# Chunked mLSTM with a feed-forward layer: the gates of four chunks in one batch on 128 partitions, and exponents, splits and state product moved behind square, copy of x and y

## The chip, the cores and the metric

The kernel runs on one core of a Trainium2 chip. The metric is the device time of one execution in microseconds, as the median of several runs. The profile is that of one execution. PE is TensorE (PEld its weight loads), DVE is VectorE, ACT is ScalarE, POOL is GpSimd, and SP is SyncE, which here issues the DMA transfers.

## The reference

For 4 batches of 8 heads (32 sequences) of 768 steps with heads of 40 numbers, an mLSTM recurrence is computed, and its output goes through a feed-forward layer of 2048 units.

```python
for t in range(S):
    m_new = np.maximum(f_gate[:, :, t] + m, i_gate[:, :, t])
    f_stab = np.exp(f_gate[:, :, t] + m - m_new)
    i_stab = np.exp(i_gate[:, :, t] - m_new)
    C = f_stab[:, :, None, None] * C + i_stab[:, :, None, None] * np.einsum('bhd,bhe->bhde', vt, kt)
    n = f_stab[:, :, None] * n + i_stab[:, :, None] * kt
    y[:, :, t] = sigmoid(o_gate) * (C @ q) / np.maximum(np.abs(n @ q), 1.0)
x = y.transpose(0, 2, 1, 3).reshape(3072, 320)
h = x @ w_in
g = np.where(h >= 1, h, np.where(h <= -1, 0.0, (h + 1) ** 2 / 4))
return g @ w_out
```

## The kernel before, in words

The sequence is cut into six chunks c of 128 steps. One chunk of one batch is a step n = 4c + b, so there are 24 steps. Within a step the recurrence is a masked product of scores and decays plus what the state brings from earlier chunks.

**Gates.** For each chunk `gate_sums` (L193), `gate_tail` (L239) and `gate_exps` (L253) turn the gates of the 32 sequences into maxima m (a scan along the 128 steps), running sums ac and al of the log decays, exponents G (for scaling v, the state and the output), nA (minus the sums, on the steps' partitions) and dec (the decay of the state). Each works on tiles of 32 partitions with 128 columns, assembles four of them in ex, and transposes ex on PE. The sums go to memory as a_d, since every step reads them back spread over 128 partitions (`load_A`, L462, tile Abc, three buffers), and dec goes through dc_d. Chunk 0 has tiles of its own in the front. Chunk 1 is begun in the front (step `g1` of the table STEPS, L55) and ended after the first group of the feed-forward layer. Chunks 2 to 5 are computed beside the feed-forward layer, a few instructions a group, from the groups 2, 13, 28 and 43 on (GATES_AT, L49).

**A step.** `prep` (L475): POOL masks Abc (`select`), ACT turns it into decays with eight exponents (`decay`, L492), POOL scales v (`scale1`). `score` (L509): PE multiplies k and q, DVE multiplies the scores with the decays (Abc again), POOL scales v once more (`scale2`). `main` (L569): PE forms C times q and the masked product, DVE adds them to hv, divides by z, multiplies with the sigmoid of the output gate (sz) and gets y; PE transposes y, ACT copies it to xh in fp32r, DVE writes the rest xl. `carry_on` (L544) forms the new state C out of a product of k and v on PE, a mask on DVE, and the old state scaled by dec on POOL. From step 8 on, except for batch 3, v and the masked scores are split into three bf16 parts on DVE and POOL (`parts3`, L149, tiles v and m).

**The feed-forward layer** goes in six blocks j of 512 rows (four steps), each of 16 groups fc. `mm1` (L674) makes eight matmuls psh of xh, xl with the split weights wh, wl, ACT applies relu and square (tile r), DVE takes maximum and minimum (r). `parts` splits r into gh (ACT) and gl (DVE), and `mm2` (L695), two groups later, makes twelve matmuls pso with oh, ol (four with the unsplit weight in block 0). A block can begin when x of its four steps is there. psh has two banks. The weights arrive as float64 words and are converted during block 0 by ACT, DVE and POOL (`words`, L309: tiles wraw, mg, win, ow).

**Order.** The front, up to the first feed-forward matmul, runs in the order of STEPS. After that the program places step n's parts at the groups that OFFS, LEAD and MLAG give (`slot`, L657), and a scheduler arranges each engine's instructions; `behind` (L416) asks for an instruction to come after one that is kept in `mark`. The engines then work through their instructions in that order.

Of the kernel before, what the change touches and what calls it, by code (L numbers as in the profile page):

```python
# [44 lines left out]
NA = 3  # L45
ST = 0


GATES_AT = (2, 13, 28, 43)  # L49
# [47 lines left out]
def mlstm_ffn_kernel(ctx, tc, qk, qn, vk, og, fi0, fi, w_in, w_out, cst, out):  # L97
# [62 lines left out]
    rst = const.tile([3 * NSEQ, L], F32, name="rst")  # L160
# [32 lines left out]
    def gate_sums(c):  # L193
# [35 lines left out]
        reset = rst[:NSEQ] if c else rst[2 * NSEQ:]  # L229
# [339 lines left out]
    def main(n):  # L569
# [21 lines left out]
        else:  # L591
            prod = [(i, k) for i in range(3) for k in range(3 - i)]
            v = parts3(t["v1"], "v3", (nc.vector, nc.gpsimd))
            for h in range(H):
                if h % 8 == 0:
                    m = parts3(M[:, h:h + 8, :], "m3", (nc.vector, nc.gpsimd))
# [20 lines left out]
        nc.vector.tensor_tensor(out=y.rearrange("p (h d) -> p h d", d=D), in0=hv[:, :, 0:D], in1=sz, op=ALU.mult)  # L617
# [114 lines left out]
    for what in STEPS.split():  # L732
# [4 lines left out]
        elif what == "Lf":  # L737
            load_gates(mid, 1, 2)
# [16 lines left out]
        elif what[0] == "g":  # L755
            run(gate_sums(n))
# [47 lines left out]
    for x in range(NG + LAG):  # L804
        j, fc = divmod(x, NFC)
        if x < NG:
# [12 lines left out]
            if x in GATES_AT:  # L819
                c = 2 + GATES_AT.index(x)  # L820
                load_gates(later, c, c + 1)
                steps = gate_steps(c)
            if x >= GATES_AT[0]:
# [17 lines left out]
_INS = ["qk", "qn", "vk", "og", "fi0", "fi", "w_in", "w_out", "cst"]  # L841


def _layout(q, k, v, i_gate, f_gate, o_gate, moe_w_in, moe_w_out):
# [22 lines left out]

    w = moe_w_in.view(np.int64)
# [26 lines left out]
```

## Time and profile before

| what | value |
|---|---|
| median of 3 runs | 540.07 us (538.07 to 540.72) |
| profiled execution, its own time | 538.07 us |
| its span, first to last instruction | 536.3 us |
| mean granted clock of PE | 0.958 |
| busy PE / DVE / ACT / POOL | 501.1 / 359.7 / 291.5 / 138.8 us |
| DMA traffic read / written | 46.67 MB / 4.04 MB |
| idle time of POOL's mask, ended by a DMA of Abc | 16.1 us in 10 waits |
| idle time of ACT's exponents, ended by POOL's mask | 37.3 us in 14 waits |
| instructions of DVE / ACT / POOL | 669 / 576 / 140 |

A row of a group or a timeline has the start in the span, the duration, engine, line, operation, output and inputs by the program's names, sizes, and in brackets the idle time of that engine just before it and what ended it. Most lines read L80 or L83, since a helper issues the instructions; the tiles tell which is which. Idle time of an engine that is not the bound costs nothing by itself. The granted clock is the share of full speed that PE was given.

### The profile page before, as it was taken

The page shows a single profiled execution, that of the slowest core. Times are in us where ns is not written, and L with a number is a line of the kernel's source. Part 1 is how long each engine was busy: PE and PEld are TensorE (multiplying, and loading weights), DVE is VectorE, ACT ScalarE, POOL GpSimd, SP SyncE. Part 2 cuts the span into 40 slices and gives each one's busy share as a digit, 9 for nine tenths or more (in the row PEclk, how much of TensorE's full clock was granted, in tenths as well). Part 3 has the DMA queues.
Part 4 walks back from the last instruction along what each step waited for, and adds up shares of the span by engine and source line. Part 5 has one row for each costly group of instructions (what it writes and reads, how often), then busy time and mean ns, then how long its engine had stood idle before and what let it go on. Part 6 is the DMA issues. An engine that isn't in the chain of part 4 may idle for free.

```text
span 536.3 us, 8899 instructions
## 1 busy us (share of the span) xinstructions
PE 501.1 (93%) x3396; PEld 427.1 (80%) x3399; DVE 359.7 (67%) x669; ACT 291.5 (54%) x576; POOL 138.8 (26%) x140
## 2 busy tenths in 40 slices
PE   8957999798997999969999979999999999999996
PEld 5735777676786889958888967988988889989986
DVE  5799997678675687748567558885566755544342
ACT  6544964555267464546636527663668444446553
POOL 3147423233352132223131232431231310000000
PEclk9987999899797999988999988999999999999999
DMA  8859454442441123233221233322243000010001
GB/s 245 264 188 303 129 172 146 149 153 91 142 134 19 41 63 103 79 88 93 51 87 56 80 113 120 74 90 77 68 149 135 19 1 2 0 38 13 1 1 50
DMA packets 29647, 51.30 MB, mean 96 GB/s; under 512 B 10124, under 2 KB 20004, under 8 KB 29604
## 3 DMA queue, kind: packets, MB, share of 16 engines
q1 hardware_dynamic: 29604, 50.72, 30.5%
q8 instruction: 27, 0.44, 0.4%
q14 instruction: 16, 0.13, 0.1%
HBM read 46.67 MB, written 4.04 MB: 95 GB/s over the span
## 4 chain that ended last, share of the span: by engine, by line
PE 75%; DVE 7%; ACT 7%; issue 3%; POOL 3%; DMA 3%; SPq 0%; ACTq 0%; POOLq 0%; DVEq 0%
PE psh L80 31%; PE pso L80 27%; PE psa L80 13%; ACT Abc L80 3%; POOL Abc L80 2%; PE psa L83 2%; DMA Abc<-a_d 2%; ACT r L80 1%; PE pso L83 1%; POOL v L80 1%; DVE r L80 1%; PE psh L83 1%; DVE win L80 1%; DVE ow L80 1%; DMA wraw<-in_w_out 1%
## 5 line engine op out<-in xcount | busy, mean ns | idle before, releaser
L80 ACT ACTIVATE r<-psh,half 128x512 f32<-128x512 f32 x96 | 65.2, 684 | 103.2 <-PE psh L80 102.9
L80 PE MATMUL psh<-xh,wh 128*128 128x512 f32 x288 | 107.4, 429 | 14.8 <-DVE r L80 12.2
L80 DVE SCALAR_TENSOR_TENSOR r<-psh,r 128x512 f32<-128x512 f32 x96 | 65.7, 686 | 80.6 <-ACT r L80 80.0
L80 PE MATMUL psh<-xh,wl 128*128 128x512 f32 x288 | 103.6, 414 | 0.0
L80 PE MATMUL pso<-ow,gh 128*128 128x320 f32 x320 | 99.4, 313 | 0.0
L80 PE MATMUL pso<-oh,gh 128*128 128x320 f32 x320 | 99.3, 313 | 0.0
L80 PE MATMUL pso<-oh,gl 128*128 128x320 f32 x320 | 93.3, 313 | 0.0
L80 DVE TENSOR_TENSOR gl<-r,gh 128x512 fp32r<-128x512 f32 x80 | 60.5, 758 | 32.4 <-ACT gh L80 31.9
L80 ACT CAST gh<-r 128x512 fp32r<-128x512 f32 x80 | 49.5, 618 | 48.9 <-DVE r L80 48.5
L80 PEld LDWEIGHTS psh<-xh,wh 128*128 128x128 f32 x288 | 53.1, 199 | 24.9 <-DVE r L80 13.9
L80 ACT ACTIVATE Abc<-Abc,nA 128x128 f32<-128x128 f32 x160 | 49.3, 390 | 37.3 <-POOL Abc L80 37.3
L80 PEld LDWEIGHTS psh<-xh,wl 128*128 128x128 f32 x288 | 56.7, 199 | 14.0 <-DVE m L83 0.4
L80 PEld LDWEIGHTS pso<-ow,gh 128*128 128x128 f32 x320 | 60.7, 190 | 3.4
L80 PEld LDWEIGHTS pso<-oh,gh 128*128 128x128 f32 x320 | 60.7, 190 | 3.3
L80 PE MATMUL psh<-xl,wh 128*128 128x512 f32 x192 | 62.7, 410 | 0.0
L80 ACT ACTIVATE r<-r 128x512 f32<-128x512 f32 x96 | 60.2, 631 | 2.4
L80 PEld LDWEIGHTS pso<-oh,gl 128*128 128x128 f32 x320 | 58.2, 188 | 0.8
L80 POOL TENSOR_TENSOR v<-vk,G 128x328 f32<-128x328 f32 x36 | 29.7, 829 | 67.2 <-issue 43.7
L80 PEld LDWEIGHTS psh<-xl,wh 128*128 128x128 f32 x192 | 37.6, 197 | 8.5
L80 POOL TENSOR_TENSOR C<-C,dec 120x369 f32<-120x369 f32 x16 | 13.7, 856 | 111.0 <-PE psa L80 111.0
L80 PE MATMUL pso<-ow,r 128*128 128x320 f32 x128 | 39.3, 452 | 0.0
L80 DVE TENSOR_TENSOR Abc<-psa,Abc 128x512 f32<-128x512 f32 x40 | 25.9, 680 | 17.8 <-PE psa L80 17.8
(187 smaller groups left out, 728.2 us busy)
## 6 DMA issues: line engine op xcount, KB each, us to landing
Abc<-a_d SPq DMA_DIRECT2D x20, 512.0 KB
raw<-in_qk SPq DMA_DIRECT2D x48, 160.0 KB
vk<-in_vk SPq DMA_DIRECT2D x20, 324.0 KB
wraw<-in_w_in SPq DMA_DIRECT2D x8, 768.0 KB
wraw<-in_w_out SPq DMA_DIRECT2D x8, 640.0 KB
sig<-in_og SPq DMA_DIRECT2D x6, 640.0 KB
out<-r SPq DMA_DIRECT2D x24, 160.0 KB
qn<-in_qn SPq DMA_DIRECT2D x20, 180.0 KB
```

What stands on the lines that cost most here:

```text
L80: r = getattr(self.engine, name)(*args, **kwargs)
L83: r = getattr(self.engine, name)(*args, **kwargs)
```

## The change

**Gates.** Chunks 1 to 4 are computed at once. The maxima scan runs once over 512 columns on 32 partitions, in the front (step `b` of STEPS, after the score product of step 1). Four transfers from SBUF to SBUF spread the maxima over 128 partitions, chunk by chunk (m_b). From there on every instruction works on 128 partitions, four chunks times 32 sequences: `batch_sums` at step `g1`, `batch_tail` and `batch_exps` after the first group. One transfer writes the sums of the four chunks to a_d, four transposes on PE replace the one of ex, and the twelve decay transfers of the four chunks go out together. The gates arrive in two forms, rows over 512 columns (fi_r) and chunks on partitions (fi_b, a new input fib). Only chunk 5 keeps the old path, from group 34 on.

**Order.** Exponents (`decay`) come behind the latest square of r and the latest copy of x. The mask (`select`) of steps from 8 on is issued one slot before the first exponents rather than in the same slot. The state product C and the splits v and m come behind the latest y.

```diff
-GATES_AT = (2, 13, 28, 43)
+JOINED = (4, 5, 6, 7)
+GATES_AT = 34
-    "x11 v1 m10 c w2 u0 m11 w2 E2 A2 x20 ...
+    "x11 v1 m10 c w2 u0 m11 b w2 E2 A2 x20 ...
+    def load_batch():
+        mb["row"] = mid.tile([NSEQ, 2, 4 * L], F32, name="fi_r")
+        nc.sync.dma_start(mb["row"], fi[:, :, L:5 * L])
+        mb["fi"] = mid.tile([P, 2, L], F32, name="fi_b")
+        nc.sync.dma_start(mb["fi"], fib)
+    def batch_maxima():
+        m = mid.tile([NSEQ, 4 * L + 1], F32, name="m_r")
+        nc.vector.tensor_copy(m[:, 0:1], carry)
+        nc.vector.tensor_tensor_scan(out=m[:, 1:], data0=mb["row"][:, 0, :], data1=mb["row"][:, 1, :], initial=m[:, 0:1],
+                                     op0=ALU.add, op1=ALU.max)
+        nc.vector.tensor_copy(carry, m[:, 4 * L:])
+        for c in range(4):
+            nc.sync.dma_start(mb["m"][c * NSEQ:(c + 1) * NSEQ], m[:, c * L:(c + 1) * L + 1])
+    def batch_sums():
...
+        nc.vector.tensor_tensor_scan(out=ac, data0=rst, data1=ah, initial=0.0, op0=ALU.mult, op1=ALU.add)
+        nc.sync.dma_start(a_d[1:5].rearrange("c s t -> (c s) t"), ac)
+    def batch_exps():
+        for q, x in enumerate((mb["fi"][:, 0, :], mb["m"][:, :L], mb["ac"], mb["ah"])):
+            nc.tensor.transpose(tp[:, q * P:(q + 1) * P], x, ident)
+        nc.scalar.activation(Gq[:, 0:3], tq[:, 0:3], AF.Exp)
+        nc.scalar.activation(Gq[:, 3], tq[:, 3], AF.Exp, scale=-1.0)
+        nc.scalar.mul(nA[:, 1:5, :], tq[:, 2], -1.0)
+        nc.scalar.activation(dx, mb["dc"].broadcast_to([P, D]), AF.Exp)
+        nc.sync.dma_start(dc_d[1:5].rearrange("c b (h d) -> (c b h) d", d=D), dx)
+        for g, h0 in enumerate(GROUPS):
+            for c in range(1, 5):
+                nc.sync.dma_start(dec[:, g, :, c], dc_d[c, :, h0 * D:(h0 + 3) * D].rearrange("b x -> x b"))
         select(n)
+        if n not in JOINED:
+            yield
         for hh in range(2):
-            decay(n, hh)
+            with behind(("r", "act"), ("x", "act")):
+                decay(n, hh)
-        nc.vector.tensor_tensor(out=Cn, ...
+        with behind("y"):
+            nc.vector.tensor_tensor(out=Cn, ...
-            v = parts3(t["v1"], "v3", (nc.vector, nc.gpsimd))
+            with behind("y"):
+                v = parts3(t["v1"], "v3", (nc.vector, nc.gpsimd))
-        y = ...
-            todo = ("prep", s0 - (LEAD if j > 1 else LEAD - 1), 3), ...
+            lead = (LEAD if j > 1 else LEAD - 1) + (n not in JOINED)
+            todo = ("prep", s0 - lead, 3 + (n not in JOINED)), ...
             if x == 0:
-                    run(gate_tail(1))
-                    gate_exps(1)
+                    batch_tail()
+                    batch_exps()
```

What this moves is shown at the start of block 2 on three engines. A row is an instruction: line, operation, output and inputs, size. On ACT before, around the copy of x (xh) of the last step that block 2 needs; Abc are the exponents, r the relu or the square, gh the cast of g:

```order
L80 CAST gh<-r 128x512
L80 ACTIVATE ex<-ah 32x128
L80 ACTIVATE Abc<-Abc,nA 128x128 x8
L80 CAST xh<-psa 128x3x128
L80 ACTIVATE r<-psh,half 128x512 x2
L80 COPY r<-pso 128x320
L80 ACTIVATE r<-r 128x512 x2
```

The same place on ACT in the changed kernel:

```order
L82 CAST gh<-r 128x512
L82 ACTIVATE r<-psh,half 128x512
L82 CAST xh<-psa 128x3x128
L82 ACTIVATE Abc<-Abc,nA 128x128 x4
L82 ACTIVATE r<-r 128x512
L82 ACTIVATE Abc<-Abc,nA 128x128 x4
L82 CAST gh<-r 128x512
```

The copy of x stood behind the eight exponents and now stands ahead of them; they have moved behind it, in two halves.

On DVE before, the work of the same step's y (hv, z, sz, y), the state product C, the split v and the rest of x (xl, xh):

```order
L80 TENSOR_TENSOR hv<-psa,hv 128x328
L80 TENSOR_TENSOR C<-psa,cs 120x369
L80 TENSOR_TENSOR v_2414<-v_2194 128x328
L80 SCALAR_TENSOR_TENSOR z<-hv,G 128x8
L80 TENSOR_TENSOR C<-C 120x369
L80 TENSOR_TENSOR z<-z,hv 128x8
L80 RECIPROCAL z<-z 128x8
L80 TENSOR_TENSOR sz<-sig,z 128x320
L80 TENSOR_TENSOR y<-hv,sz 128x320
L80 TENSOR_TENSOR xl<-psa,xh 128x2x128
```

The same on DVE in the changed kernel:

```order
L82 TENSOR_TENSOR hv<-psa,hv 128x328
L82 TENSOR_TENSOR ow<-ow,oh 128x640
L82 SCALAR_TENSOR_TENSOR z<-hv,G 128x8
L82 TENSOR_TENSOR gl<-r,gh 128x512
L82 TENSOR_TENSOR z<-z,hv 128x8
L82 RECIPROCAL z<-z 128x8
L82 TENSOR_TENSOR sz<-sig,z 128x320
L82 TENSOR_TENSOR y<-hv,sz 128x320
L82 TENSOR_TENSOR C<-psa,cs 120x369
L82 TENSOR_TENSOR v_2340<-v_2131 128x328
L82 TENSOR_TENSOR C<-C 120x369
```

C and the split of v (the next step's) stood among z, sz and y, and now follow y.

On PE before, around the transposes of that y (ident,y), the last pso matmuls of block 1 and the first psh matmuls on the new x:

```order
L80 MATMUL pso<-oh,gh 128x320
L80 MATMUL pso<-oh,gl 128x320 x3
L80 MATMUL pso<-ow,gh 128x320
L80 MATMUL pso<-oh,gl 128x320
L80 MATMUL psa<-ident,y 128x128 x3
L80 MATMUL psa<-raw 128x128
L80 MATMUL psh<-xh,wh 128x512 x2
L80 MATMUL psh<-xh,wl 128x512 x2
```

The same on PE in the changed kernel:

```order
L82 MATMUL psh<-xh,wh 128x512
L82 MATMUL psh<-xh,wl 128x512
L82 MATMUL pso<-oh,gh 128x320
L82 MATMUL psa<-ident,y 128x128 x3
L82 MATMUL pso<-ow,gh 128x320
L82 MATMUL psa<-raw 128x128
L82 MATMUL pso<-oh,gl 128x320
L82 MATMUL pso<-oh,gh 128x320
L82 MATMUL pso<-ow,gh 128x320
```

Before, all 24 pso matmuls that follow the step's state product stand ahead of the transposes, and the block's first psh matmuls follow them at once. Now 21 pso matmuls and the last two psh groups of block 1 stand between the state product and the transposes, and 23 pso matmuls between the transposes and block 2's first psh matmul.

More of the change, by code (lines that the diff above doesn't have):

```diff
@@ L96, in mlstm_ffn_kernel @@
 @with_exitstack
-def mlstm_ffn_kernel(ctx, tc, qk, qn, vk, og, fi0, fi, w_in, w_out, cst, out):
+def mlstm_ffn_kernel(ctx, tc, qk, qn, vk, og, fi0, fi, fib, w_in, w_out, cst, out):
     nc = Core(tc)
@@ L158, in parts3 @@
         return hi, mid, lo
-    rst = const.tile([3 * NSEQ, L], F32, name="rst")
+    rst = const.tile([P, L], F32, name="rst")
     nc.gpsimd.memset(rst, 1.0)
@@ new lines, in batch_sums @@
+    def batch_sums():
+        a, m = mb["fi"][:, 0, :], mb["m"]
+        ah = mb["ah"] = mid.tile([P, L], F32, name="ah_b")
+        ac = mb["ac"] = mid.tile([P, L], F32, name="ac_b")
+        nc.vector.tensor_tensor(out=a, in0=a, in1=m[:, :L], op=ALU.add)
+        nc.vector.tensor_tensor(out=a, in0=a, in1=m[:, 1:], op=ALU.subtract)
+        nc.vector.tensor_scalar(out=ah, in0=a, scalar1=CLAMP, scalar2=GRID, op0=ALU.max, op1=ALU.add)
+        nc.vector.tensor_scalar(out=ah, in0=ah, scalar1=-GRID, scalar2=None, op0=ALU.add)
+        nc.vector.tensor_tensor_scan(out=ac, data0=rst, data1=ah, initial=0.0, op0=ALU.mult, op1=ALU.add)
+        nc.sync.dma_start(a_d[1:5].rearrange("c s t -> (c s) t"), ac)
+        nc.vector.scalar_tensor_tensor(out=a, in0=a, scalar=CLAMP, in1=ah, op0=ALU.max, op1=ALU.subtract)
@@ new lines, in batch_tail @@
+    def batch_tail():
+        i, m, ah, ac = mb["fi"][:, 1, :], mb["m"], mb["ah"], mb["ac"]
+        b = mb["fi"][:, 0, :]
+        al = ah
+        nc.vector.tensor_tensor_scan(out=al, data0=rst, data1=b, initial=0.0, op0=ALU.mult, op1=ALU.add)
+        nc.vector.tensor_tensor(out=b, in0=i, in1=m[:, 1:], op=ALU.subtract)
+        nc.vector.tensor_tensor(out=b, in0=b, in1=al, op=ALU.subtract)
+        dh = m[:, :L]
+        nc.vector.tensor_tensor(out=dh, in0=ac[:, L - 1:].broadcast_to([P, L]), in1=ac, op=ALU.subtract)
+        nc.vector.tensor_tensor(out=dh, in0=dh, in1=b, op=ALU.add)
+        nc.vector.tensor_tensor(out=dh, in0=dh, in1=al[:, L - 1:].broadcast_to([P, L]), op=ALU.add)
+        mb["dc"] = mid.tile([P, 1], F32, name="dc_b")
+        nc.vector.tensor_tensor(out=mb["dc"], in0=ac[:, L - 1:], in1=al[:, L - 1:], op=ALU.add)
@@ L616, in main @@
         y = wk.tile([P, DM], F32, name="y", bufs=2)
-        nc.vector.tensor_tensor(out=y.rearrange("p (h d) -> p h d", d=D), in0=hv[:, :, 0:D], in1=sz, op=ALU.mult)
+        mark["y"] = nc.vector.tensor_tensor(out=y.rearrange("p (h d) -> p h d", d=D), in0=hv[:, :, 0:D], in1=sz, op=ALU.mult)
         if 0 < c < NC - 1:
@@ L647, in mlstm_ffn_kernel @@
         if j:
-            todo = ("prep", s0 - (LEAD if j > 1 else LEAD - 1), 3), ("score", s0, 2), ("main", s0 + MLAG, 3)
+            lead = (LEAD if j > 1 else LEAD - 1) + (n not in JOINED)
+            todo = ("prep", s0 - lead, 3 + (n not in JOINED)), ("score", s0, 2), ("main", s0 + MLAG, 3)
         else:
@@ L755, in mlstm_ffn_kernel @@
         elif what[0] == "g":
-            run(gate_sums(n))
+            if n:
+                batch_sums()
+            else:
+                run(gate_sums(n))
+        elif what[0] == "b":
+            batch_maxima()
         elif what[0] == "k":
@@ L818, in mlstm_ffn_kernel @@
                         pass
[L819 to L823, printed above, removed]
+            if x == GATES_AT:
+                load_gates(later, NC - 1, NC)
+                steps = gate_steps(NC - 1)
+            if x >= GATES_AT:
                 with tc.issue_after(mark["r", "dve"].ins):
```

22 lines of the change are left out of this document (15 added, 7 removed), and 2 rows, old and new, of the table STEPS.

## The prediction

> **What bounds the kernel now.** I read the page, then TensorE's waits, then stretches of the span, then single instructions.
>
> ```profile
> span 536.3 us, 8899 instructions
> PE 501.1 (93%) x3396; PEld 427.1 (80%) x3399; DVE 359.7 (67%) x669; ACT 291.5 (54%) x576; POOL 138.8 (26%) x140
> ```
>
> TensorE (PE) is busy for 501.1 of 536.3 us, so any gain here has to come out of the 35.2 us of idle time, or out of time in which its clock is reduced. Both lie in a few stretches. The columns are the stretch, its length, busy time of PE, weight loads, VectorE (DVE), ScalarE (ACT) and GpSimd (POOL), the granted clock, DMA share and GB/s.
>
> ```profile
> 31.00:44.00 13.00, 5.89 (x17) 4.14 (x18) 12.53 (x25) 6.62 (x12) 7.50 (x5) 0.76 0.77 260
> 98.00:105.00 7.00, 4.03 (x25) 3.31 (x25) 6.51 (x11) 2.12 (x6) 2.01 (x3) 0.82 0.54 171
> 105.00:119.00 14.00, 13.92 (x72) 11.43 (x73) 11.03 (x25) 7.24 (x16) 4.93 (x5) 0.84 0.48 147
> 119.00:145.00 26.00, 22.82 (x111) 17.77 (x110) 19.42 (x36) 10.91 (x26) 8.92 (x9) 0.87 0.40 128
> 145.00:161.00 16.00, 15.36 (x133) 13.16 (x131) 12.25 (x26) 9.76 (x16) 8.74 (x5) 1.00 0.45 139
> 161.00:181.00 20.00, 16.70 (x85) 14.19 (x84) 11.41 (x23) 13.19 (x28) 3.20 (x4) 0.83 0.07 11
> 222.00:242.00 20.00, 15.71 (x95) 13.07 (x95) 12.27 (x23) 8.20 (x19) 6.77 (x6) 0.91 0.36 112
> 242.00:305.00 63.00, 63.00 (x495) 55.74 (x494) 42.85 (x81) 35.91 (x73) 17.29 (x18) 0.97 0.24 71
> 305.00:327.00 22.00, 17.48 (x113) 14.71 (x111) 13.79 (x29) 9.71 (x23) 5.87 (x7) 0.92 0.35 107
> 327.00:400.00 73.00, 73.00 (x569) 65.55 (x570) 53.08 (x93) 45.16 (x89) 23.05 (x22) 0.98 0.32 97
> ```
>
> Idle time is length less PE's busy time; what the clock costs is length times what the clock lacks to 1. That gives six terms. (b) 31 to 44: 7.1 us idle. (c) 98 to 119: 3.05 idle and 2.2 of clock, 5.3. (d) 119 to 145: 3.2 and 3.4, 6.6. (e) 145 to 181: 3.9 and 3.4, 7.3. (f) 222 to 305: 4.3 and 3.7, 8.0. (g) 305 to 400: 4.5 and 3.2, 7.7. A dip of the clock follows each wait, so a wait costs nearly twice its length. Terms (c) to (g) hold 34.9 us.
>
> **What makes the waits.** Term (f), at the start of block 2; columns are start, length, engine, line, operation, tiles:
>
> ```profile
> 225.49 0.53 DVE L80 TENSOR_TENSOR C<-psa,cs 120x369 f32<-120x369 f32 x1
> 226.87 0.70 DVE L80 TENSOR_TENSOR z<-z,hv 128x8 f32<-128x8 f32 x1
> 227.84 1.41 DVE L80 TENSOR_TENSOR sz<-sig,z 128x320 f32<-128x320 f32 x1
> 229.28 0.49 DVE L80 TENSOR_TENSOR y<-hv,sz 128x320 f32<-128x320 f32 x1
> 227.81 1.09 POOL L80 TENSOR_SCALAR_AFFINE_SELECT Abc<-Abc 128x1024 f32<-128x1024 f32 x1 [0.27 <-DMA vk<-in_vk]
> 228.94 2.45 ACT L80 ACTIVATE Abc<-Abc,nA 128x128 f32<-128x128 f32 x8 [4.52 <-POOL Abc L80]
> 231.29 0.45 ACT L80 CAST xh<-psa 128x384 fp32r<-128x384 f32 x1
> 229.92 0.52 PE L80 MATMUL psa<-ident,y 128*128 128x128 f32 x3 [2.17 <-DVE y L80]
> 231.80 0.88 PE L80 MATMUL psh<-xh,wh 128*128 128x512 f32 x2 [0.94 <-ACT xh L80]
> ```
>
> Two things hold PE up. DVE runs the state product C and the bf16 split of v before it finishes y, and z and sz stretch beside POOL's work. Then ACT stands 4.52 us in front of eight exponents whose mask POOL has not written yet, and the copy of x, which the block's first matmul needs, is queued behind them. Term (g) is the same picture one block on:
>
> ```profile
> 315.83 0.52 PE L80 MATMUL psa<-ident,y 128*128 128x128 f32 x3 [2.31 <-DVE y L80]
> ```
>
> Terms (d) and (e) show the other half of it:
>
> ```profile
> 132.20 2.67 PE L80 MATMUL psa<-v,Abc 128*128 128x41 f32 x16 [1.93 <-DVE xh L80]
> 155.73 4.72 POOL L80 TENSOR_SCALAR_AFFINE_SELECT Abc<-Abc 128x1024 f32<-128x1024 f32 x1 [3.17 <-DMA Abc<-a_d]
> 160.48 0.99 ACT L80 ACTIVATE Abc<-Abc,nA 128x128 f32<-128x128 f32 x3 [2.16 <-POOL Abc L80]
> 164.81 1.22 PE L80 MATMUL psh<-xh,wh 128*128 128x512 f32 x2 [3.30 <-DVE r L80]
> ```
>
> ACT waits for a mask, the relu and square behind it come late, DVE's r comes late, and PE has no free bank.
>
> **The change part by part.** *Order of exponents, mask, C and splits: terms (c) to (g).* Exponents now stand behind the square and the copy of x, the mask of steps from 8 on is issued a slot earlier, C and the splits stand behind y. The program's order shows it at block 2: C and the v split follow y, the copy of x precedes the exponents, and PE has 21 pso matmuls and two psh groups of eight between the state matmuls and the transposes, and 23 pso matmuls between those and the first matmul on the new x. A group of eight and the twelve pso matmuls that go with it last
>
> ```profile
> 520.90 1.86 PE psh L80 x8
> 522.76 1.75 PE pso L80 x12
> ```
>
> so y now has two times 1.86 and 21 times 1.75/12 us of work to cover it, 6.8 us, and the copy of x 23 times 1.75/12, 3.4 us. From C at 225.49 to the end of y at 229.77 DVE took 4.3 us with the work that now goes behind; the way from the transposes to the first matmul took 1.9. Both are covered, so I take three quarters of (f) and of (g): -6.0 and -6.0. The quarter left is for what comes late next, the score product and its split. Block starts (d) and (e) lose the same cause, but there the weight conversions share DVE, ACT and POOL, and a step's mask can still come late; I take half: -3.3 and -3.5. Bounds for each of the four are nothing and the whole term.
>
> Term (c) begins with the gates of chunk 2 and the queue of SP:
>
> ```profile
> 85.46 1.34 DMA dc_d<-dx
> 88.76 4.10 DMA Abc<-a_d
> ```
>
> The load of the sums for step 7 stood behind the decay transfers of that chunk. These are gone from there, which frees the 3.3 us from 85.46 to 88.76; of 5.3 I take -3.0, bounds 0 and -5.3.
>
> *Gates in a batch.* Four chunks at 128 partitions take as many instructions as one did at 32, so three sets go. On DVE they lie where PE is bound, except at the start, term (b):
>
> ```profile
> 34.36 1.23 DVE L83 TENSOR_TENSOR_SCAN m<-fi_t,m 32x128 f32<-32x128 f32 x1
> 36.36 1.55 DVE L83 TENSOR_TENSOR fi_t<-fi_t,m 32x128 f32<-32x128 f32 x2
> 41.51 0.40 DVE L83 TENSOR_TENSOR_SCAN ah<-rst,fi_t 32x128 f32<-32x128 f32 x1
> 42.72 0.69 DVE L80 SCALAR_TENSOR_TENSOR r<-psh,r 128x512 f32<-128x512 f32 x1
> 43.46 1.22 PE L80 MATMUL psh<-xh,wh 128*128 128x512 f32 x2 [6.80 <-DVE r L80]
> ```
>
> DVE is full here and PE waits for r. The maxima scan goes to the front, and the last scan stands behind the first r: 1.23 and 0.40 less ahead of r, 1.6 at most; the two subtractions stay, though earlier. I take -1.5, bounds 0 and -1.6.
>
> The front pays: a scan over 512 columns ahead of the first z, at most four times 0.40, 1.6 us, overhead counted four times, which leaves room for its two one-column copies.
>
> ```profile
> 17.76 0.49 DVE L83 TENSOR_TENSOR y<-psh,sz 128x320 f32<-128x320 f32 x1
> 19.24 0.53 PE L83 MATMUL psa<-ident,y 128*128 128x128 f32 x3
> ```
>
> y ends at 18.25 and PE takes it at 19.24, so 1.0 of it is hidden: +0.6, bounds 0 and +1.6. The four transfers of maxima leave when that scan ends, near 20, and are first read at about 32; at 4.1 us, the longest row above, 8 us are left. SP holds its later loads until then, and the batch's rows add 0.2 MB to the front; both I take at nothing, bound 1 us. The twelve decay transfers go out in a row:
>
> ```profile
> 55.78 0.36 SPq L80 DMA_DIRECT2D wraw<-in_w_in  x1
> 62.44 0.36 SPq L80 DMA_DIRECT2D wraw<-in_w_out  x1
> 87.72 0.93 SPq L80 DMA_DIRECT2D dec<-dc_d  x2
> ```
>
> 12 by 0.47 is 5.6 us of SP, and SP has 6.3 between the weight loads at 55.78 and 62.44, where the order now puts them: nothing, or up to 5.6 on a late weight conversion if that gap is taken. On ACT the batch's exponents and negation read 640 columns where one chunk had 160; by three exponents of 128 columns in 0.99 us that is at most 1.2 more, once, while PE has first-block matmuls to run: nothing, bound 1.2.
>
> *A new wait.* At block starts 1 to 3 four exponents (half of 2.45) now precede casts of g that the second matmuls need: 1.2 each, three times, +3.7; bounds 0 and, if the mask is late as at 155.73, +3.6 more each.
>
> On that mask: it took 4.72 us against 1.09 at 227.81. [...]
>
> Sum: +0.6 -1.5 -3.0 -3.3 -3.5 -6.0 -6.0 +3.7 = -19.0. Against the profiled execution's own 538.07 (span 536.3 and 1.8 around it) that is 519.1. The median of the runs stands 2.0 above that execution, so the new median should lie between 519 and 521: 520.0. A measurement of this kernel can tell about 0.5%, 2.7 us, from no change.
>
> **Rivals.** *The clock stays low.* Waits shorten, but shorter ones still bring the clock down. For it: the clock lost 3.4 us in 119 to 145, whose longest wait is 1.93. Against it: from 145 to 161 PE was idle for 0.6 in all and the clock stayed at 1.00. Then only the idle shares of what I took go: 1.7, 1.6, 2.0, 3.2 and 3.4 of (c) to (g), 11.9; with the rest 538.07 +0.6 -1.5 -11.9 +3.7 = 529.0. Chance 0.22. [...]
>
> *All of it goes.* 538.07 -34.9 -1.6 +0.6 = 502.2; needs the conversions never to be late. Chance 0.08.
>
> *The wait only moves.* ACT waits for the same mask one place on, before the next relu; POOL's queue, which decides when the mask is ready, loses only small copies. Then 538 to 539. For it: in (e) POOL itself is the releaser. Chance 0.08.
>
> *Slower.* The exponents stand behind square and copy; if by that the score products, y and x of a block's last step come one group later than the matmuls that cover them, PE stands a group, 1.86 + 1.75 = 3.6 us, at each of four block starts: +14.4, less (b) and (c), plus the front: 538.07 +14.4 -4.5 +0.6 = 548.6. It decides where less than y's 4.3 us of matmuls stand ahead of the transposes. Against it: at block 2 they are 6.8. Chance 0.06.
>
> My forecast has 0.56, its own range 511 to 526. The range 507 to 534 adds the first rival and part of the second. Faster by over 0.5%: the forecast, the first two rivals and a little of the third, 0.87; same 0.07; slower 0.06.
>
> **What would show it.** After: PE's waits for y and xh at the starts of blocks 2 and 3 gone, and the clock at 1.00 there; ACT's wait for Abc from POOL, if still there, with the copy of x ahead of it; the first r near 41; PE idle 17 to 22 us instead of 35. Wrong if PE is idle as long as before, if new waits of over 2 us for gh stand at block starts, or if the first matmul on x still waits.

## The result and the profile after

The changed kernel takes 518.22 us (median of 4 runs, 517.07 to 519.29), the kernel before, beside it, 539.07 (537.19 to 540.72). The ratio is 0.961, 95% interval 0.957 to 0.966: faster. Here and below a median and a range are of all runs, while a ratio leaves out the few that took over 1.5% longer than the fastest of the same kernel, such as the 529.76 us in e4. The profiled execution of after took 517.97 us, 20.1 less than that of before. First its page:

```profile
span 516.2 us, 8817 instructions
PE 490.7 (95%) x3396; PEld 419.4 (81%) x3399; DVE 343.0 (66%) x621; ACT 289.1 (56%) x560; POOL 135.9 (26%) x136
```

PE is idle for 25.5 us instead of 35.2, and it is busy for 10.4 us less with the same number of matmuls. The clock accounts for that: its mean is 0.979 instead of 0.958, and busy time times clock is 480 us in both. The stretches show where; the columns are those of the prediction's table:

```profile
31.00:46.00 15.00, 7.02 (x22) 4.75 (x22) 14.11 (x27) 6.14 (x10) 5.98 (x6) 0.81 0.69 219
98.00:119.00 21.00, 17.86 (x96) 14.38 (x92) 16.83 (x31) 10.84 (x25) 6.71 (x7) 0.84 0.53 166
119.00:145.00 26.00, 24.08 (x142) 19.30 (x141) 21.62 (x38) 9.15 (x20) 11.65 (x12) 1.00 0.49 150
181.00:290.00 109.00, 108.77 (x841) 96.84 (x840) 78.53 (x146) 63.30 (x126) 34.07 (x33) 1.00 0.27 79
290.00:320.00 30.00, 28.38 (x223) 25.18 (x222) 20.27 (x37) 20.87 (x42) 8.85 (x9) 1.00 0.40 127
320.00:400.00 80.00, 79.56 (x611) 70.69 (x610) 52.62 (x95) 46.95 (x92) 21.92 (x20) 1.00 0.28 90
```

From 119 to 400 us the clock stands at 1.00, and from 181 to 400 PE is idle for 2.3 us. From 119 to 145 that is partly this execution: e5 below, which differs only in the place of two loads, has 0.93 there, as have most of the other changed kernels. The beginning has hardly changed: from 31 to 46 PE is still idle for 8.0 us, and 98 to 119 has 3.1 idle and a clock of 0.84, where before had 3.05 and 0.84.

To see what each place gave, the same instructions are set side by side. Before, the first matmul on x, a step's product of k and q, and the first matmul of block 3 (the other marks stand in the prediction):

```profile
31.31 1.22 PE L80 MATMUL psh<-xh,wh 128*128 128x512 f32 x2 [0.57 <-ACT xh L83]
152.28 0.94 PE L80 MATMUL psa<-raw 40*128 40x128 f32 x12 [0.59 <-DVE hv L80]
317.70 1.22 PE L80 MATMUL psh<-xh,wh 128*128 128x512 f32 x2 [0.94 <-ACT xh L80]
```

After, all six marks in order:

```profile
33.56 1.65 PE L82 MATMUL psh<-xh,wh 128*128 128x512 f32 x3 [0.57 <-ACT xh L85]
45.20 1.22 PE L82 MATMUL psh<-xh,wh 128*128 128x512 f32 x2 [6.12 <-DVE r L82]
131.92 1.28 PE L82 MATMUL psa<-v,Abc 128*128 128x41 f32 x10 [0.79 <-DVE xh L82]
149.32 0.94 PE L82 MATMUL psa<-raw 40*128 40x128 f32 x12 [0.59 <-DVE hv L82]
220.05 0.62 PE L82 MATMUL psh<-xh,wh 128*128 128x512 f32 x2
298.29 0.62 PE L82 MATMUL psh<-xh,wh 128*128 128x512 f32 x2
```

| stretch between marks | before | after | change | forecast |
|---|---|---|---|---|
| start to first matmul on x | 31.31 | 33.56 | +2.25 | +0.6 |
| to PE's return after the first r | 12.15 | 11.64 | -0.5 | (b) -1.5 |
| to the masked product near 132 | 88.74 | 86.72 | -2.0 | (c) -3.0 |
| to the product of k and q near 150 | 20.08 | 17.40 | -2.7 | (d) -3.3 |
| to block 2 | 79.52 | 70.73 | -8.8 | (e) and the wait of (f) |
| to block 3 | 85.90 | 78.24 | -7.7 | clock of (f), wait of (g) |
| to the end of the span | 218.60 | 217.91 | -0.7 | clock of (g) |

The first four rows give 3.0 us where the sum had 7.2, and the last three give 17.1 where it had 3.5 + 6.0 + 6.0, less 3.7 for the new waits, 11.8. The total was met by two errors of opposite sign, so that it came so close is luck.

At block 2, what was said of the waits is seen: DVE finishes y ahead of C and the split, and ACT copies x ahead of the exponents.

```profile
212.07 0.49 DVE L82 TENSOR_TENSOR y<-hv,sz 128x320 f32<-128x320 f32 x1
212.48 0.54 DVE L82 TENSOR_TENSOR C<-psa,cs 120x369 f32<-120x369 f32 x1
215.74 0.49 PE L82 MATMUL psa<-ident,y 128*128 128x128 f32 x3
216.38 0.47 ACT L82 CAST xh<-psa 128x384 fp32r<-128x384 f32 x1
216.74 1.28 ACT L82 ACTIVATE Abc<-Abc,nA 128x128 f32<-128x128 f32 x4
```

y ends at 212.56 and PE takes it at 215.74 without a wait; x is copied at 216.85, and PE needs it at 220.05. In the page's groups ACT's exponents no longer wait for the mask (the last column is the idle time ahead of them, 37.3 us before):

```profile
L82 ACT ACTIVATE Abc<-Abc,nA 128x128 f32<-128x128 f32 x160 | 49.9, 391 | 0.2
```

What is new are the waits for gh and gl, in the step to block 1 and in block 3:

```profile
155.53 0.42 PE L82 MATMUL pso<-oh,gh 128*128 128x320 f32 x1 [0.51 <-ACT gh L82]
158.96 0.42 PE L82 MATMUL pso<-oh,gl 128*128 128x320 f32 x1 [1.64 <-DVE gl L82]
312.52 0.41 PE L82 MATMUL pso<-oh,gh 128*128 128x320 f32 x1 [1.62 <-ACT gh L82]
```

ACT's row of work ahead of the last of them shows what the cast stood behind:

```profile
306.82 1.28 ACT L82 ACT_TABLE_LOAD   x1
308.11 1.27 ACT L82 ACTIVATE sig<-sig 128x1280 f32<-128x1280 f32 x1
309.39 1.28 ACT L82 ACT_TABLE_LOAD   x1
310.68 1.28 ACT L82 ACTIVATE Abc<-Abc,nA 128x128 f32<-128x128 f32 x4
311.87 0.60 ACT L82 CAST gh<-r 128x512 fp32r<-128x512 f32 x1
```

The four exponents are 1.28 of it; the sigmoid with a table load on each side is another 3.8. The wait for gl at 157 goes through DVE: ahead of gl it waited 2.32 us for ACT's cast oh, which stood behind four exponents too.

### The profile page after: what moved, and what is told of

It is laid out like the page before. It is cut to its first block, busy times and chain, and to the rows that moved or that the text cites. A ratio compares the mean times of both kernels' runs of the same rounds, so it can differ in the third digit from the quotient of the medians.

```text
span 516.2 us, 8817 instructions
## 1 busy us (share of the span) xinstructions
PE 490.7 (95%) x3396; PEld 419.4 (81%) x3399; DVE 343.0 (66%) x621; ACT 289.1 (56%) x560; POOL 135.9 (26%) x136
## 4 chain that ended last, share of the span: by engine, by line
PE 85%; DVE 6%; ACT 5%; DMA 3%; issue 1%; SPq 0%; ACTq 0%; DVEq 0%
PE pso L82 33%; PE psh L82 33%; PE psa L82 15%; ACT Abc L82 1%; PE pso L85 1%; DMA raw<-in_qk 1%; ACT L82 1%; PE psa L85 1%; DVE ow L82 1%; DMA wraw<-in_w_in 1%; PE psh L85 1%; ACT r L82 1%; DVE win L82 1%; DMA out<-r 1%; ACT sig L82 0%
## 5 line engine op out<-in xcount | busy, mean ns | idle before, releaser
L82 DVE SCALAR_TENSOR_TENSOR r<-psh,r 128x512 f32<-128x512 f32 x96 | 65.8, 686 | 71.5 <-ACT r L82 71.3
L82 PE MATMUL psh<-xh,wh 128*128 128x512 f32 x288 | 104.3, 418 | 6.7 <-DVE r L82 6.1
L82 PE MATMUL pso<-oh,gh 128*128 128x320 f32 x320 | 100.6, 317 | 2.4 <-ACT gh L82 2.1
L82 PE MATMUL psh<-xh,wl 128*128 128x512 f32 x288 | 99.8, 401 | 0.0
L82 DVE TENSOR_TENSOR gl<-r,gh 128x512 fp32r<-128x512 f32 x80 | 62.2, 779 | 40.5 <-ACT gh L82 40.4
L82 PEld LDWEIGHTS psh<-xh,wl 128*128 128x128 f32 x288 | 55.2, 192 | 13.1 <-DVE wl L85 0.4
L82 PEld LDWEIGHTS psh<-xh,wh 128*128 128x128 f32 x288 | 51.8, 194 | 15.2 <-DVE r L82 6.8
L82 POOL TENSOR_SCALAR_AFFINE_SELECT Abc<-Abc 128x1024 f32<-128x1024 f32 x20 | 25.4, 1275 | 48.3 <-DMA Abc<-a_d 46.1
L82 POOL TENSOR_TENSOR m<-m 128x1024 bf16<-128x1024 f32 x12 | 24.4, 2037 | 46.4 <-DVE m L82 46.4
```

The costliest lines, as they stand in the source:

```text
L82: r = getattr(self.engine, name)(*args, **kwargs)
```

## The experiments

The theory to be tested is the prediction's: waits for y (DVE's order) and for x (ACT's order) are each about half of what is lost at the block starts, and the batch adds the terms at the start. Rivals: one part does nearly all; the batch does more than its own terms; one part alone only moves the waits.

### The parts one by one

**e1: the batch alone.** The three edits of the order are undone:

```diff
-        if n not in JOINED:
-            yield
         for hh in range(2):
-            with behind(("r", "act"), ("x", "act")):
-                decay(n, hh)
+            decay(n, hh)
...
-        with behind("y"):
-            nc.vector.tensor_tensor(out=Cn, ...)
+        nc.vector.tensor_tensor(out=Cn, ...)
```

(the two splits likewise). Expected:

> The changed kernel with all three order edits undone (exponents, mask, C and splits placed as before), the gates still in one batch. Theory (the order edits bring the terms at block starts 2 and 3, the batch brings the rest): the waits for y and for the copy of x at those block starts are back, 12 to 14 us of the 20.9, so 531 to 535. Rival (fewer gate instructions on DVE, ACT and POOL bring it all): 518 to 522.

Measured: 529.89 us (529.13 to 531.75), ratio to before 0.986 (0.981 to 0.991), 7.9 less than the 537.79 of before in the same group of runs, and between the two expectations. The prediction's terms for the batch come to +0.6 - 1.5 - 3.0 = -3.9, so alone the batch does more. The waits for y at blocks 2 and 3 are not back. It would be natural to say that DVE, with fewer gate instructions, finishes y sooner, but the trace of block 2 doesn't bear that out. Before, DVE's last wait ahead of y ends at 222.74, and behind it come 0.8 us of a chunk's gates (the third, a copy, is left out here):

```profile
222.74 0.69 DVE L80 SCALAR_TENSOR_TENSOR r<-psh,r 128x512 f32<-128x512 f32 x1 [1.00 <-ACT r L80]
223.35 0.27 DVE L80 SCALAR_TENSOR_TENSOR fi_t<-fi_t,ah 32x128 f32<-32x128 f32 x1
223.66 0.41 DVE L80 TENSOR_TENSOR_SCAN ah<-rst,fi_t 32x128 f32<-32x128 f32 x1
```

In e1 the conversion of a weight stands in the same place:

```profile
213.60 0.82 DVE L82 TENSOR_TENSOR ow<-ow,oh 128x640 fp32r<-128x640 f32 x1
219.51 0.49 DVE L82 TENSOR_TENSOR y<-hv,sz 128x320 f32<-128x320 f32 x1
```

From DVE's last wait to the end of y it takes 7.0 us in both, 222.74 to 229.77 and 212.99 to 220.00. What differs is PE's order. The state product (v,vk) ahead of y, before and in e1, and the transposes of y in e1:

```profile
223.38 0.87 PE L80 MATMUL psa<-v,vk 128*120 128x123 f32 x6
214.00 0.87 PE L82 MATMUL psa<-v,vk 128*120 128x123 f32 x6
221.50 0.49 PE L82 MATMUL psa<-ident,y 128*128 128x128 f32 x3
```

Before, 24 pso matmuls stand between that product and the transposes, and PE is through with them 4.4 us after the product began; in e1 21 pso and two groups of psh stand there, 7.5 us, and y is ready in time. The same reckoning for the kernels below, block 2 / block 3, in us from the start of the state product:

| kernel | y ends | PE is through with its other matmuls | PE's wait for y |
|---|---|---|---|
| before | 6.4 / 6.3 | 4.4 / 4.2 | 2.17 / 2.31 |
| exponents alone (e11) | 6.0 / 4.6 | 4.4 / 4.4 | 1.69 / 0.35 |
| C and splits alone (e10) | 3.2 / 3.2 | 5.8 / 2.7 | 0 / 0.65 |
| both (e2) | 4.3 / 4.0 | 5.2 / 4.3 | 0 / 0 |
| batch alone (e1) | 6.0 / 4.6 | 7.5 / 6.5 | 0 / 0 |
| after | 4.3 / 3.1 | 7.5 / 6.8 | 0 / 0 |

So the order of C and the splits brings y forward, and the batch comes with more matmuls ahead of the transposes: 6.3 to 7.8 us in all four of these kernels that have it (e3 and e4 are the others), 2.7 to 5.8 in the four without. Either covers the wait, but for 0.65 us in e10. Why the scheduler places the groups so with the batch is not shown.

In e1 other waits appear: 1.44 us for y at the start of block 1 (161 us), and two for r, 2.98 at 399, where ACT works on eight exponents around the relu, and 2.46 at 466.

**e2: the order alone.** The gates of before, with the three edits of the order added to them (e1's diff the other way round, on before). Expected:

> The kernel before with the three order edits alone, gates chunk by chunk. Theory: block starts 2 and 3 without waits, first block as before: 525 to 529. Rival (the gate instructions are what counts): 535 to 540.

Measured: 520.88 us (520.09 to 522.44), ratio 0.969 (0.964 to 0.974), 16.9 less than before; better than expected. e1 and e2 make 24.8 together, the whole change about 20. Each of these gains is uncertain by 2 to 3 us, so the times alone hardly show that they overlap; the table above does, since the waits for y at blocks 2 and 3 are gone in both.

**e3: batch and exponents.** The changed kernel with C and the splits free of y. Expected:

> The changed kernel with C and the splits free again to stand ahead of y; exponents still behind square and copy of x. Theory (y and the copy of x are two waits of about the same size at each block start): half of the 13 us of the block starts is lost, 523 to 527, with PE waiting for y but not for the copy. Rival (the copy of x behind late exponents is the whole of it): 518 to 520.

Measured: 524.61 us (523.04 to 526.02), ratio 0.976 (0.970 to 0.983). The time is as expected, the way there is not: PE does not wait for y at blocks 2 and 3, as in e1, and the longest waits after the first r are 2.73 for gl at 157, 1.77 for hv near 103 (as in after) and 1.60 for gh at 315. PE is idle for 29.3 us against 25.5 in after.

**e4: batch and y.** The changed kernel with exponents and mask as before. Expected:

> The changed kernel with exponents and mask placed as before; C and the splits still behind y. Theory: half of the block starts is lost, 523 to 527, ACT waits for the mask again with the copy of x behind it. Rival (y alone was late): 518 to 520.

Measured: 519.77 us (517.63 to 529.76), ratio 0.966 (0.960 to 0.971). This is the rival, that y alone was late. ACT waits 28.9 us for masks again, in 16 waits, and this costs little: the result lies 1.6 above the changed kernel, whose runs overlap with it. The edit of the exponents can't be told from nothing by these times once the other two are there.

**e10: C and splits behind y, alone, on before.**

```diff
-        nc.vector.tensor_tensor(out=Cn, ...)
+        with behind("y"):
+            nc.vector.tensor_tensor(out=Cn, ...)
...
-            v = parts3(t["v1"], "v3", (nc.vector, nc.gpsimd))
+            with behind("y"):
+                v = parts3(t["v1"], "v3", (nc.vector, nc.gpsimd))
```

(and the split of m). Expected:

> The kernel before, with C and the splits of v and m behind y and nothing else: gates, exponents and masks stand as before. Reference points: before 538 to 539, both order edits on before 520.9. Theory (DVE's order ahead of y makes the waits at block starts 2 and 3, and the place of the exponents adds little): 521 to 527, PE without a wait at 230 and 316 although ACT still waits over 4 us for the mask there. Rival, the prediction's own picture (y and the copy of x are each half of it): PE still waits for xh behind the masked exponents, 529 to 535. Rival two (a part alone only moves the wait to later blocks, as the batch alone did): waits of 2 to 3 us at other block starts, 530 to 536.

Measured: 524.98 us (524.45 to 527.18), ratio 0.979 (0.973 to 0.985), 12.8 less than before: the first theory. Two lines of its expectation failed: PE still waits 0.65 us for y at block 3, and ACT's wait for the mask at block 2 is 1.51 us, not over 4.

```profile
221.62 2.45 ACT L80 ACTIVATE Abc<-Abc,nA 128x128 f32<-128x128 f32 x8 [1.51 <-POOL Abc L80]
224.62 0.42 PE L80 MATMUL pso<-oh,gh 128*128 128x320 f32 x1 [1.45 <-ACT gh L80]
```

The wait has a new victim: the cast of gh stands behind all eight exponents. It is the wait that the change has with four of them.

**e11: exponents behind square and copy of x, alone, on before** (the first two pieces of e1's diff, added to before, with the mask a slot earlier). Expected:

> The kernel before, with the exponents behind square and copy of x and the mask of steps from 8 on a slot earlier, and nothing else: C and the splits stand ahead of y as before. Reference points: before 537.8, C and splits behind y alone 525.0, both 520.9. Theory (the order of DVE is the larger part; the exponents are worth what they added to the other, 4 to 5): 532 to 535, PE still waiting for y at block starts 2 and 3. Rival, the prediction's picture (copy of x and y each half): 527 to 531, no wait of ACT for the mask and no wait of PE for xh, a wait for y of 2 us at each start.

Measured: 534.53 us (530.71 to 536.78), ratio 0.996 (0.992 to 0.999): 2.7 less. The time is the theory's. At block 2 the wait for x has shrunk and the wait for y stands, but at block 3 the wait for y has nearly gone too, which was not expected:

```profile
221.29 0.52 PE L82 MATMUL psa<-ident,y 128*128 128x128 f32 x3 [1.69 <-DVE y L82]
222.38 0.72 PE L82 MATMUL psh<-xh,wh 128*128 128x512 f32 x2 [0.15 <-ACT xh L82]
302.83 0.52 PE L82 MATMUL psa<-ident,y 128*128 128x128 f32 x3 [0.35 <-DVE y L82]
```

Before, these waits are 2.17, 0.94 and 2.31. In their place PE waits 1.16 us for gl at 322 and 1.55 and 2.46 for r at 393 and 466, so part of what is gained comes back later. The profile is of the fastest of the ten executions, 530.71 us. What the mask's earlier slot is worth by itself is not shown; it was not run alone.

| gain over before in the same group of runs, us | without the batch | with the batch |
|---|---|---|
| neither edit of the order | 0 | 7.9 |
| exponents | 2.7 | 13.2 |
| C and splits behind y | 12.8 | 18.0 |
| both | 16.9 | 19.7 to 20.9 |

The last cell is e5 (below), whose instructions differ from after's only in the place of two loads, and after itself. Each gain is uncertain by 2 to 3 us. Taken as they stand, the exponents are worth 1.7 to 5.3 us, C and the splits 6.5 to 14.2 and the batch 2.8 to 10.5, by what else has been changed already.

### The front and the first wait

**e5: the batch's rows loaded later.** In the profile of after PE waits 0.79 us at 7.9 us for a load of q and k, and the front runs late from there.

```diff
-    "Lg Li Lo Lq0 Lv0 Lq1 Lw0 Lf Lq2 Lv2 Lq3 ...
+    "Lg Li Lo Lq0 Lv0 Lq1 Lw0 Lq2 Lv2 Lf Lq3 ...
```

Expected:

> The changed kernel, with the two loads of the batch's gate rows issued behind the next q, k and v loads. Theory (the 0.2 MB ahead of them delay the load of raw, PE waits 0.2 to 0.8 us for it near 8 us in every kernel with the batch and in none without it): that wait gone, 0.5 to 2 less, 516.2 to 517.7. Rival (when a load lands varies from execution to execution, and the front catches up before the first matmul of block 0): no change, 518.2 within 0.5.

Measured: 518.08 us (516.95 to 518.61), ratio 0.965 (0.961 to 0.969): the rival, no change. The wait for the load is gone, the first matmul on x comes at 33.03 instead of 33.56, and in place of the load PE waits 0.92 us for the first y. The load was not what set the front.

**e12: the scan of the maxima behind the second y.** Only the place of three DVE instructions changes.

```diff
-    "... m10 c w2 u0 m11 b w2 E2 A2 x20 ... w2 s3 v3 y1 x31 ...
+    "... m10 c w2 u0 m11 w2 E2 A2 x20 ... w2 s3 v3 y1 b x31 ...
```

Expected:

> The changed kernel, with the scan of the batch's maxima moved on DVE from ahead of the first z to behind the second y, where DVE stood 2.3 to 2.5 us for ACT. Theory (the scan, 1.27 to 1.82 us, holds up the first y and with it the front, as the waits for y of 0.70 and 1.38 at 20 to 21 us in two of the experiments say): 0.7 to 1.4 less than the changed kernel, 516.8 to 517.5, and no wait for y near 20. Rival (the front is bound by the load of raw, the scan lies beside it): no change, 518.2 within 0.5; if the maxima now come late for the batch's sums, up to 1 more.

Measured: 516.80 us (516.39 to 517.12), ratio 0.963 (0.959 to 0.966). Against e5 on the same chip it is 1.3 us less, and only one of e5's six runs lies in the range of e12's: the theory. The first y is no longer waited for, though PE waits 1.09 us for loads of q and k here, and the first matmul on x comes at 32.22. What the scan did where it stood is seen in e4, where PE then waits 1.38 us for the first y:

```profile
17.36 1.82 DVE L85 TENSOR_TENSOR_SCAN m_r<-fi_r,m_r 32x512 f32<-32x512 f32 x1
```

Over all profiled kernels, the first matmul on x comes at 31.2 to 31.8 without the batch (before, e2, e10, e11), at 32.3 to 34.1 with the scan ahead of the first z (after, e1, e3 to e6, e14), and at 31.0 to 32.2 with the scan moved (e12, e13, e15).

**e14: the batch's sums behind the first r.** Six DVE instructions, 2.2 us in after, and the loads of the sums that depend on them.

```diff
-    "w2 u2 z1 y2 w2 u3 t1 z2 y3 w2 t2 z3 t3 d g1 "
+    "w2 u2 z1 y2 w2 u3 t1 z2 y3 w2 t2 z3 t3 d "
...
-        for n in range(4, 4 + NA):
-            load_A(n)
...
                 with tc.issue_after(mark["r", "dve"].ins):
+                    batch_sums()
+                    for n in range(4, 4 + NA):
+                        load_A(n)
                     batch_tail()
```

Expected:

> The changed kernel with the batch's sums (six instructions of DVE, 0.28 + 0.81 + 0.21 + 0.23 + 0.42 + 0.27 = 2.2 us ahead of the first r) and the loads of the sums for steps 4 to 6 behind the first r. Theory (the wait of 6.1 us for the first r is DVE's count of work ahead of it): the wait 3.9 to 4.2, the time 516 to 516.5. Rival (those conversions stretch beside POOL's, whatever else DVE does): first r less than 1 us earlier, 517.5 to 518.5. Rival two (the sums reach the masks too late): first r earlier, but PE waits later, for exponents or r between 50 and 110 us, 518.5 to 522.

Measured: 520.12 us (518.33 to 523.40), ratio 0.971 (0.966 to 0.975): not better than the changed kernel. DVE had less to do ahead of r and stood still for part of it instead, 0.90 and 0.78 us:

```profile
39.23 0.96 DVE L82 TENSOR_TENSOR wl<-win,wh 128x768 fp32r<-128x768 f32 x1 [0.90 <-ACT wh L82]
41.37 0.61 DVE L82 TENSOR_SCALAR win<-wraw 128x768 uint16<-128x768 uint16 x1 [0.78 <-DMA wraw<-in_w_in]
41.87 1.62 DVE L82 SCALAR_TENSOR_TENSOR ow<-mg,ow 128x640 int32<-128x640 int32 x1
44.27 1.22 PE L82 MATMUL psh<-xh,wh 128*128 128x512 f32 x2 [5.80 <-DVE r L82]
```

r stands in DVE's queue behind the weights' conversion, and that waits for ACT's cast and for the weights' load; the conversion ow takes 1.62 us, of which more below. The wait for r is 5.80 against 6.12: that is the first rival's. The time lies in the second rival's range, but the later waits that it named are not there, PE's waits between 50 and 110 us being no longer than in after. The clock from 119 to 145 is 0.93, but so it is in eight other profiles of changed kernels, and only after and e12 have 1.00. What makes the median 1.9 us longer than after's stays open.

### The new wait, and versions of the change

**e6: exponents also behind the latest cast of gh.**

```diff
-            with behind(("r", "act"), ("x", "act")):
+            with behind(("r", "act"), ("x", "act"), ("g", "act")):
                 decay(n, hh)
...
-        nc.scalar.copy(gh, r)
+        mark["g", "act"] = nc.scalar.copy(gh, r)
```

Expected:

> The changed kernel, with the exponents also behind the latest cast of gh. Theory (the waits of 0.50, 1.64 and 1.62 us for gl and gh at 155, 157 and 311 are the exponents and the two table loads ahead of those casts, and nothing else is late): the three waits gone, 3.8 less, 514 to 516. Rival (the exponents are needed soon after, so the score product, y or the next relu comes late in their place): the waits move and the time stays, 517.5 to 521.

Measured: 516.67 us (514.75 to 520.20), ratio 0.963 (0.958 to 0.968). The three waits are gone; a wait for y near 387 has grown from 0.39 to 1.19. The highest of the six runs is the profiled one, in which the granted clock, outside its dips, lay at 0.95 from 52 to 290 us and at 0.929 in the mean, where the other five have 0.975 to 0.983, so its other stretches can't be set beside after's; the other five took 514.75 to 517.14. The gain over e5 is 1.4 by the medians, less than the 3.8 of the waits removed: between theory and rival.

**e13: e6 and e12 together; e15: e6, e12 and e14 together.** Expected of e13:

> The changed kernel with both of the edits that gained alone: the scan of the maxima behind the second y (516.8) and the exponents behind the latest cast of gh (516.7 with its profiled execution, 514.8 to 517.1 without). Theory (they lie at different places and add): 518.2 - 1.4 - 1.5 to 2 = 514.8 to 515.3. Rival (the earlier front is given back at the waits of block 0 for weights and gates): 516 to 517.

Measured: 515.54 us (514.99 to 516.64), ratio 0.962 (0.958 to 0.967), between the theory and the rival. Expected of e15:

> The changed kernel with all three: maxima behind the second y, sums behind the first r, exponents behind the latest cast of gh. Theory (each term is its own): 514.8 to 515.3 less what the late sums gain alone, 513 to 515. Rival (late sums and late exponents together make the masks and score products late): 516 to 521.

Measured: 516.56 us (515.60 to 517.92), ratio 0.964 (0.959 to 0.968): the rival's 516 to 521. The late sums bring no gain here either; its runs overlap with e13's. e13 has the lowest median of all, 2.7 below after, and the two kernels' runs do not overlap. But it ran beside a before of 537.26 and after beside one of 539.07, and by the ratios, 0.962 and 0.961, they can't be told apart. That e13 beats the change is likely from e6 and e12, not shown.

## Why the prediction was right, and where it was wrong

The forecast was 520.0 us; the result is 518.2. The direction, the place (block starts 2 and 3) and the returning clock were right. Several terms were not, and that the sum came so close is luck. Step by step:

- **Waits for y and x at blocks 2 and 3, and the clock there: right in place, too small in size.** All of it went, where three quarters were taken. The quarter kept for "what comes late next" was too careful: no score product or split came late. But the 6.8 us of matmuls that were counted as cover for y come with the batch, not with the order: with the order alone PE has 5.2 and 4.3 us, with the batch alone 7.5 and 6.5 (table under e1).
- **"Then ACT stands 4.52 us in front of eight exponents": its weight was wrong.** ACT's wait for the mask was the longest idle time in the rows, and most of it was off the path. e4 keeps 28.9 us of it and lies within 1.6 us of after; e11 takes the exponents away from the copy of x and gains 2.7 of 537. DVE's order alone gave 12.8 (e10). The row to go by was PE's: 2.17 for y, only 0.94 for xh.
- **The batch, -3.9: near in number, wrong in place.** On top of both edits of the order it gives 2.8 to 4.0 (e2 against e5 and after), but not at the start, where it was taken: from the start to the product of k and q e2 needs 149.25 us and after 149.32, from there to block 3 e2 needs 152.8 and after 149.0. What the prediction left out is that with the batch PE's matmuls are placed otherwise; that is what removes the waits at blocks 2 and 3 in e1, where the batch alone gave 7.9. "On DVE they lie where PE is bound" was not the error: at block 2 DVE's stretch ahead of y is 7.0 us with the gates and without.
- **The front: mis-sized.** +0.6 was taken, bounds 0 and +1.6. The profile of after has +2.25, of which 0.5 is likely that execution's late load (e5); with the scan ahead the first matmul comes 1.7 later on average than without the batch (33.2 against 31.5 over the kernels above). The scan took 1.27 us in after, within four times 0.40, but up to 1.82 in the runs, with two copies of 0.14, and the 1.0 us counted as cover was not there: PE waits 0.70 to 1.38 for that y in the profiles of e1, e3 to e6 and e14, not in after's.
- **(b): failed.** -1.5 was taken for DVE instructions removed ahead of the first r. In after PE returned 0.5 earlier relative to the block's start, but from the first matmul on x to that return it is 11.7 us on average in the four profiles without the batch and 11.7 in the six that have the scan and the sums where the change has them: nothing was gained. In after DVE does not stand still ahead of r. Three of its conversions, mg, win and ow, took 1.43, 1.49 and 1.64 us where before they took 0.53, 0.92 and 0.80, and one took 0.60 for 1.48, together 1.4 more, which eats what was removed. The long ones began while POOL was at work on an instruction (begun at 35.41, 37.36 and 42.35 in after, at 39.71 before), the last of after's here, first after, then before:

```profile
42.35 1.45 POOL L82 TENSOR_SCALAR win<-wraw 128x768 uint16<-128x768 uint16 x1 [3.30 <-DMA wraw<-in_w_in]
42.79 1.64 DVE L82 SCALAR_TENSOR_TENSOR ow<-mg,ow 128x640 int32<-128x640 int32 x1
41.88 0.80 DVE L80 SCALAR_TENSOR_TENSOR ow<-mg,ow 128x640 int32<-128x640 int32 x1
41.95 1.52 POOL L80 TENSOR_SCALAR ow<-wraw 128x640 uint16<-128x640 uint16 x1 [0.80 <-DMA wraw<-in_w_out]
```

In after POOL had 1.0 us left when DVE's began, and DVE's took 0.84 longer. Before, DVE's began first, and it was POOL's that took longer, 1.52 against 0.92 at 45.49 in after. Between 30 and 100 us no such conversion of before or after is lengthened that does not overlap an instruction of POOL: ow from mg took 0.80 or 0.81 in the four places without one and 0.80 to 1.66 in the six with one. Overlap alone does not lengthen one; win from mg took 0.92 beside POOL at 35.51 before, and 0.94 without POOL at 69.09. With 2.2 us less of DVE's work (e14) ow again took 1.62 and DVE stood still besides.
- **(c): near in number, wrong in cause.** -3.0 was taken for the decay transfers of chunk 2; the stretch from r to 132 is 2.0 shorter. But the waits between 98 and 119 are as long as before, 3.1 us, and the batch, which removes those transfers, leaves the whole stretch as it was: 88.9 in e1 against 88.7 before. Where the exponents are moved without the batch it is 86.0 (e11) and 86.5 (e2), and after has 86.7. Of the waits before it is those at 65.8, 120.4 and 132.2 that have gone or shrunk (0.86, 0.68, and 1.93 to 0.79). The term itself was also added up too small: by its own rule the stretch 98 to 105 lacks another 1.3 us of clock, so (c) is 6.6 and not 5.3.
- **(d): -2.7 for -3.3, partly by this execution.** e5, the same instructions but for two loads, has 19.0 us there, 1.1 less than before, like e1, e2 and e11; only after and e12 have 17.4, with the clock at 1.00 where the others have 0.93.
- **The new wait: right in size.** +3.7 was taken for three casts of gh; the waits are 0.51, 1.64 and 1.62, 3.8 together. It lay at two places instead of three, the 1.64 came by way of gl and the cast of a weight, and at block 3 two table loads and a sigmoid stood ahead of the cast too. Removing it gained 1.4, so part of it had covered something else.
- **The rival of the clock: fell in its time; its premise, that shorter waits still bring the clock down, is not settled.** From 181 to 400 the clock was back. Waits of 1.64 and 1.62 in after left it at 1.00. But it was not the length of a wait that decided it, as the last section shows.
- **"If the mask is late as at 155.73, +3.6 more each": did not come.** The longest of after's 20 masks takes 1.97 us and their median is 1.13, where before had one of 4.72, and ACT's exponents wait 0.2 us in all.
- **The signs that were named:** the waits for y and xh went and the clock came back, as said. PE's idle time is 25.5 us and not 17 to 22, and the first r begins at 44.46 and not near 41; the latter goes back to the front and to (b).

What was not foreseen is that the batch and the order of C and the splits cover the same waits. By the times, the three gains alone sum to 7.9 + 12.8 + 2.7 = 23.4 and together they give about 20, which is no more than their uncertainty; the overlap is shown by the waits in e1, e2 and e10.

## What to carry to other kernels

When an engine waits at a block start, take two times from one event ahead of it: when the awaited result is ready, and when the waiting engine is through with its other work. An edit can move either, and two edits that each cover the wait do not add there. To count the instructions that are taken off an engine is not enough: without the gates DVE's stretch ahead of y was as long as with them, and it was PE's order that had changed. A sum that comes out proves none of its terms; the same marks set side by side, in more than one kernel, show which of them hold. An idle time in front of an instruction tells nothing about the path until the bound engine's own wait names it; ACT's 37 us of waiting for masks was worth 1.7 to 5.3 us. And an engine that is busy nearly all the time ahead of a late result need not be the cause: take work off it, and see whether it stands still instead, or its instructions get longer, as DVE did ahead of r in e14 (0.90 and 0.78 us of standing still, and 1.62 for ow).

## What the runs showed of the hardware

**The clock did not follow the length of a wait.** In e1 a wait of 2.98 us was followed by no dip and one of 2.46, 67 us later, by half clock (the clock is the third number from the right); its windows after each:

```profile
402.00:404.00 2.00, 2.00 (x9) 1.65 (x10) 1.96 (x5) 1.16 (x3) 0.00 (x0) 1.00 0.00 0
470.00:472.00 2.00, 2.00 (x7) 1.71 (x7) 0.30 (x1) 0.76 (x2) 0.00 (x0) 0.50 0.21 69
```

In e14 a dip came where the two nearest waits are 0.81 and 0.72 us (in the 8 us from 98 to 106 PE is idle for 2.4 in all):

```profile
102.00:104.00 2.00, 1.41 (x13) 1.44 (x13) 1.92 (x6) 0.47 (x1) 0.66 (x1) 1.00 0.66 230
104.00:106.00 2.00, 1.28 (x9) 0.94 (x8) 1.93 (x5) 0.45 (x1) 1.32 (x1) 0.62 0.78 240
106.00:108.00 2.00, 2.00 (x15) 1.77 (x15) 1.89 (x6) 1.08 (x2) 0.45 (x2) 0.50 0.91 279
```

The prediction's "a dip of the clock follows each wait" is therefore not a rule. What brings a dip is not shown; ahead of the one in e14 PE was not idle throughout, but busy for 2.7 of the 4 us from 102 to 106.

**A third level of the clock, beside the 1.00 and the 0.50 above.** In the profiled execution of e6 the clock stood at 0.95 in the undisturbed stretches from 52 to 290 us, here in one without a wait of note, where after has 1.00:

```profile
181.00:290.00 109.00, 108.78 (x838) 96.89 (x837) 79.20 (x144) 64.69 (x129) 34.38 (x31) 0.95 0.26 78
```

What set it is not known. In the same window the thirteen other profiles have 1.00, but for 0.97 in before and 0.98 in e11, where PE was idle for 4.3 and 3.5 us.

**A scan's time goes less with its columns than expected.** On 32 partitions, 128 columns took 0.40 and 512 took

```profile
18.20 1.27 DVE L85 TENSOR_TENSOR_SCAN m_r<-fi_r,m_r 32x512 f32<-32x512 f32 x1
```

so by an estimate from these two it is 2.3 ns a column, (1.27 - 0.40) / 384, and 0.11 us besides; 128 columns on 128 partitions took 0.42 in after. In e4 the same 512 columns took 1.82, and the 128 columns of the maxima took 1.23 before, at 34.36, beside an instruction of POOL (33.16 to 35.38). But the 1.27 of after ran beside two of POOL's (17.56 to 20.00) as well, so what made the others longer is not shown.
